# An FFT with a SiLU network on one core: first steps in direct form, later weights prepared between them

## The chip, the cores and the metric

One core of one Trainium2 chip runs the kernel in one launch. The metric is the device time in microseconds. Three runs of the kernel before took 938.07, 939.1 and 939.98 us; the median is 939.1.

## The reference

```python
X = np.fft.fft(np.fft.fft(x, axis=1), axis=2).real   # x: (4, 3008, 256)
x = X.astype(np.float32).reshape(4 * 3008, 256)
h = x @ w_in                                         # w_in: (256, 2048)
g = h * (1.0 / (1.0 + np.exp(-h)))
out = (g @ w_out).astype(np.float32)                 # w_out: (2048, 256)
```

Both weights are float64. The kernel gets their 64-bit words and makes float32 of them itself.

## The kernel before, in words

The Fourier transform over the 256 columns is folded into w_in: eight quarters q of 256 columns of w_in are each converted (`to_f32`, L66: an absolute value on ACT, then four passes on DVE), multiplied by a small matrix dft on PE (`project`, L415, eight products), and split into a part that is exact in the short format (abh, `large`, L423, on ACT) and a remainder (abl, `small`, L432, on DVE). `large` also takes one row out of the product, sends it by a DMA to a128, and sets that row to zero. The Fourier transform over the 3008 rows is done by products with tables (te, to, t2) in 16 chunks of 376 or 378 output rows, four kinds of chunk for each of the four batches. Each chunk needs an operand (`operand`, L194: sums and differences of folded x), a transform on PE (L255), and `spread` (L291), which copies the transform into uvh and uvl and sends its row 0 to all partitions as ub.

A chunk then goes through 16 steps f, one for 128 hidden columns. `first` (L309) makes two products u and v with six matmuls; `act` (L324) makes p = ub * a128 + u, p + v and p - v on DVE, which are h for a row and for its mirror row, and Silu and a short copy gh on ACT; gl = h - gh is a DVE pass in `rest` (L344), for chunk 0 a POOL pass in `act` (L341). `second` (L351), three steps later (LAG), multiplies by w_out with twelve matmuls into four accumulators, which `o` copies out after the last step.

All instructions of an engine run in the order in which the program writes them. Before the loop, a startup (L439 to L507) is written out by hand: loads of w_in and x on SyncE's queue, the second half of x added by a POOL DMA, tables by POOL, and the eight quarters, the first sums of x and the transform of chunk 0 laced into each other. Quarters 6 and 7 are projected there and copied in steps 0 and 1. In chunk 0, w_out's eight pieces are converted between the steps, one in two steps, by generators that `act` advances (`fill`). Two lists of generators, one for DVE work and one for POOL work (`queue`, `pool_queue`), are advanced a little at the end of each step by `drain`, with a budget; `plan` says at which step something is put on them. A tile of a pool with a tag has as many buffers as `bufs` says; a new one waits until the oldest is read.

Of the kernel before, what the change touches and what calls it, by code (L numbers as in the profile page):

```python
# [48 lines left out]
def fft_mlp(ctx, tc, x1, x2, w_in, w_out, te, to, t2, rot1, rot2, dft, out):  # L49
# [38 lines left out]

    def load_wo(q):

        wo_raw[q] = fold_p.tile([128, 2, D], I64, tag="ri0", name="wo", bufs=2)
        nc.sync.dma_start(out=wo_raw[q], in_=w_out[q * 256:(q + 1) * 256, :].rearrange("(f p) d -> p f d", p=128))  # L92

    def convert_wo(q):
        wf = fold_p.tile([128, 2, D], F32, tag="half", name="wf", bufs=3)
# [3 lines left out]
        yield
        tt(wl, wf, wh.bitcast(F32), op=ALU.subtract)  # L100

    def start_wo(q):
        wo_work[q] = convert_wo(q)
        next(wo_work[q])
# [293 lines left out]
    late = ctx.enter_context(ExitStack())  # L398
    with ExitStack() as start:
        st = start.enter_context(tc.tile_pool(name="st", bufs=1))  # L400
        wr = start.enter_context(tc.tile_pool(name="wr", bufs=3))
        ps = late.enter_context(tc.tile_pool(name="ps", bufs=2, space=PSUM))
        dft_sb = st.tile([128, 2, 2, 128], F32, name="dft_sb")
        win, wf32, pws, conv = {}, {}, {}, {}

        def load_w(q):
            win[q] = wr.tile([128, 2, 256], I64, tag="win", name="win", bufs=7)
            nc.sync.dma_start(out=win[q], in_=w_in[:, q * 256:(q + 1) * 256].rearrange("(c p) f -> p c f", p=128))

        def ahead(q):  # L410
            wf32[q] = wr.tile([128, 2, 256], F32, tag="wf", name="wf", bufs=3)
            conv[q] = to_f32(win.pop(q), wf32[q])
            next(conv[q])

        def project(q):  # L415

            w = wf32.pop(q)
            pw = pws[q] = pq_tile() if q in (1, 3, 5) else ps.tile([128, 2, 512], F32, tag="ps", name="pw")
            for m in range(2):
                for c in range(2):  # L420
                    nc.tensor.matmul(pw[:, m, :256], dft_sb[:, c, m, :], w[:, c], start=c == 0, stop=c == 1)

        def large(q):  # L423
            fs = slice(q * 256, (q + 1) * 256)
            pool, tag = (st, "row") if q < 6 else (fold_p, "half")
            row = pool.tile([1, 128, 2], F32, tag=tag, name="row", bufs=3)
            nc.scalar.activation(row, pws[q][0:1, 1, :256].rearrange("o (f p) -> o p f", p=128), AF.Copy)
            nc.sync.dma_start(out=a128[q], in_=row)
            nc.scalar.activation(pws[q][0:1, 1, :256], zero, AF.Copy)
            nc.scalar.activation(abh[:, :, fs], pws[q][:, :, :256], AF.Copy)  # L430

        def small(q):  # L432
            fs = slice(q * 256, (q + 1) * 256)
            tt(abl[:, :, fs], pws.pop(q)[:, :, :256], abh[:, :, fs].bitcast(F32), op=ALU.subtract)

        def load_tables(n, t):
            nc.gpsimd.dma_start(out=tabs[n], in_=t)

        load_w(0)  # L439
        load_w(1)  # L440
        nc.scalar.dma_start(out=dft_sb, in_=dft)
        nc.gpsimd.memset(zero, 0.0)
        warm = st.tile([1, 1], F32, name="warm")
        nc.scalar.activation(warm, zero[:, :1], AF.Silu)
        load_x(1, 0, lo)
        load_w(2)
        load_x(0, 0)
        add_x(1, 0, lo)
        add_x(0, 0)
        load_tables("t2", t2)  # L450
        for q in range(3, 8):
            load_w(q)
        nc.sync.dma_start(out=rot_sb[0], in_=rot1)
        nc.sync.dma_start(out=rot_sb[1], in_=rot2)
        load_wo(0)
        load_wo(1)

        ahead(0)
        ahead(1)
        run(conv.pop(0))  # L460
        project(0)
        ahead(2)
        run(conv.pop(1))
        large(0)
        project(1)
        run(conv.pop(2))
        large(1)
        small(0)
        project(2)
        ahead(3)  # L470
        run(first_sums(1, lo))
        large(2)
        small(1)
        small(2)
        run(conv.pop(3))
        project(3)
        ahead(4)
        large(3)
        run(first_sums(0))
        op = operand(0)  # L480
        for _ in range(3):
            next(op)
        run(conv.pop(4))
        run(op)
        project(4)
        po = pq_tile()
        ahead(5)
        ahead(6)
        large(4)
        small(3)  # L490
        run(conv.pop(5))
        transform(0, po)
        small(4)
        project(5)
        ahead(7)
        run(conv.pop(6))
        spread(0, po)
        project(6)
        large(5)
        small(5)  # L500
        run(conv.pop(7))
        project(7)
        load_tables("te", te)
        load_tables("to", to)
        start_wo(0)
        run(wo_work.pop(0))
        start_wo(1)  # L507
# [41 lines left out]
    for n in range(len(steps) + LAG):  # L549
# [6 lines left out]
        if n < len(steps):  # L556
# [6 lines left out]
        if n == 0:
            large(6)
            large(7)
        elif n == 1:
            small(6)
            small(7)
# [6 lines left out]
        if n < len(steps):  # L575
# [109 lines left out]
```

## Time and profile before

| | |
|---|---|
| median of three runs | 939.1 us |
| profiled execution, own time | 938.11 us |
| its span | 936.3 us |
| PE busy | 885.2 us, 95% |
| PEld busy | 873.0 us, 93% |
| DVE busy | 756.4 us, 81% |
| ACT busy | 534.4 us, 57% |
| POOL busy | 196.0 us, 21% |
| mean PE clock granted | 0.974 |

The span is the time from the first to the last instruction of one profiled execution. Busy times are shares of it; an engine can be far from busy over the whole span and still hold up a stretch of it. The clock is given as a share of 2.4 GHz; the lower of the two levels, 1.2 GHz, shows as 0.5.

### The profile page before, as it was taken

Reading aid. Unit: us, or ns where it says so; the run is one execution under the profiler, and the core shown is the slowest. Engines: PE = TensorE matmul, PEld = TensorE weight load, DVE = VectorE, ACT = ScalarE, POOL = GpSimd, SP = SyncE. Lnnn points to the kernel's source line nnn. Section 1 sums busy time; section 2 is a strip of 40 time slices with the busy share of each in tenths; the row PEclk is TensorE's granted clock in tenths of the full one; section 3 lists DMA queues with packets and bytes.
Section 4 is the critical chain, followed back from the end, with each engine's and each line's share of the span. In section 5 each row is a group of like instructions: output and inputs, shape, how many; then the busy total and the mean of one; then the engine's idle time right before and its main releaser. Section 6 shows DMA issues by size and latency. Waiting matters only on the chain.

```text
span 936.3 us, 12926 instructions
## 1 busy us (share of the span) xinstructions
PE 885.2 (95%) x5008; PEld 873.0 (93%) x5008; DVE 756.4 (81%) x1215; ACT 534.4 (57%) x738; POOL 196.0 (21%) x214
## 2 busy tenths in 40 slices
PE   3569979999989999999999999999999999999998
PEld 2458869999989999999999999999999999999998
DVE  5689868797877979797987879797887978797785
ACT  3245566565674656575755646475655656565554
POOL 1016562165040106080200106130000101010000
PEclk9579989999999999999999999999999999999999
DMA  9631311532102045210302033110302020120300
GB/s 268 250 54 41 55 36 25 78 78 8 35 0 23 21 95 127 7 37 1 42 1 10 34 54 79 6 37 1 42 1 9 34 9 34 5 38 1 43 1 34
DMA packets 19709, 40.96 MB, mean 44 GB/s; under 512 B 3264, under 2 KB 13504, under 8 KB 17728
## 3 DMA queue, kind: packets, MB, share of 16 engines
q1 hardware_dynamic: 18192, 30.12, 18.1%
q0 software_dynamic: 1312, 9.76, 4.5%
q8 instruction: 39, 0.64, 0.3%
q10 hardware_dynamic: 144, 0.26, 0.1%
q14 instruction: 22, 0.18, 0.1%
HBM read 24.70 MB, written 12.34 MB: 40 GB/s over the span
## 4 chain that ended last, share of the span: by engine, by line
PE 83%; DVE 7%; DMA 3%; ACT 2%; POOL 2%; issue 1%; SPq 1%; DVEq 0%; POOLq 0%; ACTq 0%
PE acc L360 17%; PE acc L365 17%; PE acc L361 17%; PE pq L317 9%; PE pq L316 9%; PE pq L315 9%; PE pq L269 5%; DMA a<-row 1%; DMA win<-in_w_in_dram 1%; SPq L92 1%; DVE h L328 1%; DVE h L331 1%; DVE wf L81 1%; DVE wf L79 1%; DVE h L332 1%
## 5 line engine op out<-in xcount | busy, mean ns | idle before, releaser
L338 ACT ACTIVATE h<-h 128x752 f32<-128x752 f32 (+2 forms) x258 | 213.8, 829 | 300.4 <-DVE h L332 298.0
L360 PE MATMUL acc<-gh,woh 128*128 128x376 f32 (+1 forms) x1024 | 345.6, 337 | 8.2 <-ACT o L373 5.4
L361 PE MATMUL acc<-gh,wol 128*128 128x376 f32 (+1 forms) x1024 | 345.0, 337 | 1.1 <-DVE wol L100 1.1
L349 DVE TENSOR_TENSOR gl<-h,gh 128x752 fp32r<-128x752 f32 (+2 forms) x242 | 236.4, 977 | 7.6 <-ACT gh L339 7.4
L365 PE MATMUL acc<-gl,woh 128*128 128x376 f32 (+1 forms) x1024 | 227.6, 336 | 0.0
L339 ACT ACTIVATE gh<-h 128x752 fp32r<-128x752 f32 (+2 forms) x258 | 214.2, 830 | 8.2
L328 DVE SCALAR_TENSOR_TENSOR h<-ub,a,pq 128x376 f32<-128x376 f32 (+1 forms) x256 | 154.6, 604 | 60.8 <-PE pq L317 58.7
L360 PEld LDWEIGHTS acc<-gh,woh 128*128 128x128 f32 x1024 | 194.0, 189 | 10.1 <-ACT o L373 5.7
L361 PEld LDWEIGHTS acc<-gh,wol 128*128 128x128 f32 x1024 | 194.5, 190 | 2.2 <-DVE wol L100 2.2
L365 PEld LDWEIGHTS acc<-gl,woh 128*128 128x128 f32 x1024 | 182.8, 190 | 0.0
L315 PE MATMUL pq<-uvh,abh 128*128 128x376 f32 (+1 forms) x512 | 173.6, 339 | 6.1 <-DVE h L332 5.7
L317 PE MATMUL pq<-uvh,abl 128*128 128x376 f32 (+1 forms) x512 | 173.1, 338 | 0.0
L316 PE MATMUL pq<-uvl,abh 128*128 128x376 f32 (+1 forms) x512 | 172.7, 337 | 0.0
L332 DVE TENSOR_TENSOR h<-h,pq 128x376 f32<-128x376 f32 (+1 forms) x256 | 140.1, 547 | 8.8
L331 DVE TENSOR_TENSOR h<-h,pq 128x376 f32<-128x376 f32 (+1 forms) x256 | 139.9, 546 | 8.4
L247 POOL TENSOR_TENSOR xl<-xf,xh 128x256 fp32r<-128x256 f32 x53 | 48.9, 948 | 325.5 <-ACT xh L240 157.5
L315 PEld LDWEIGHTS pq<-uvh,abh 128*128 128x128 f32 x512 | 97.4, 190 | 8.7 <-DVE h L332 7.6
L316 PEld LDWEIGHTS pq<-uvl,abh 128*128 128x128 f32 x512 | 97.5, 191 | 0.1
L317 PEld LDWEIGHTS pq<-uvh,abl 128*128 128x128 f32 x512 | 97.5, 190 | 0.0
L303 DVE TENSOR_TENSOR uvl<-pq,uvh 128x752 fp32r<-128x752 f32 (+1 forms) x16 | 15.1, 943 | 59.1 <-ACT uvh L302 59.1
L189 POOL TENSOR_TENSOR ri<-ri,raw 128x256 f32<-128x256 f32 (+1 forms) x28 | 26.0, 942 | 137.9 <-ACT ri L185 137.6
L341 POOL TENSOR_TENSOR gl<-h,gh 128x752 fp32r<-128x752 f32 x16 | 30.0, 1876 | 76.4 <-ACT gh L339 72.6
(83 smaller groups left out, 482.6 us busy)
## 6 DMA issues: line engine op xcount, KB each, us to landing
out_dram<-o SPq DMA_DIRECT2D x48, 188.0 KB, 2.3
raw<-in_x_dram SPq DMA_DIRECT2D x5, 1024.0 KB, 11.0
raw<-in_x_dram POOLq DMA_DIRECT2D x5, 1024.0 KB, 9.5
win<-in_w_in_dram SPq DMA_DIRECT2D x8, 512.0 KB, 13.7
wo<-in_w_out_dram SPq DMA_DIRECT2D x8, 512.0 KB, 4.0
out_dram<-o SPq DMA_DIRECT2D x16, 189.0 KB, 2.5
ub<-row SPq DMA_DIRECT2D x12, 188.0 KB, 8.5
t<-in_t_dram POOLq DMA_DIRECT2D x1, 1128.0 KB, 13.8
```

The lines of the kernel that those rows point to most:

```text
L315: nc.tensor.matmul(po, abh[:, i, fs], uvh[:, i, :n], start=True, stop=False)
L316: nc.tensor.matmul(po, abh[:, i, fs], uvl[:, i, :n], start=False, stop=False)
L317: nc.tensor.matmul(po, abl[:, i, fs], uvh[:, i, :n], start=False, stop=True)
L328: stt(p[:, :n], ub[:, :n], a128[f // 2][:, f % 2:f % 2 + 1], pq[:, 0, :n], op0=ALU.mult, op1=ALU.add)
L331: tt(h[:, 0, :n], p[:, :n], pq[:, 1, :n], op=ALU.add)
L332: tt(h[:, 1, :n], p[:, :n], pq[:, 1, :n], op=ALU.subtract)
L338: nc.scalar.activation(h[:, sg, :n], h[:, sg, :n], AF.Silu)
L339: nc.scalar.activation(gh[:, sg, :n], h[:, sg, :n], AF.Copy)
L349: tt(gl[:, sg, :n], g[:, sg, :n], gh[:, sg, :n].bitcast(F32), op=ALU.subtract)
L360: nc.tensor.matmul(po, wo[0][f // 2][:, f % 2, es], gh[:, sg, :n], start=f == 0, stop=False)
L361: nc.tensor.matmul(po, wo[1][f // 2][:, f % 2, es], gh[:, sg, :n], start=False, stop=False)
L365: nc.tensor.matmul(accs[c][i][:, :n], wo[0][f // 2][:, f % 2, es], gl[:, sg, :n], start=False, stop=f == NF - 1)
```

## The change

In the first eight steps of chunk 0 (`DIRECT = 8`), `first` makes h of both signs on PE by twelve matmuls: the first operand with v and with -v (vneg, made by ACT in `spread`). Row 0 of the second part keeps its sign (turn) and abh keeps the row in which a128 was taken (not set to zero for quarters 0 to 3), so DVE's three passes and a128 are not used there; ACT's Silu reads the products. After step 8 the row is set to zero in abh and abl by POOL.

```diff
+        if c == 0 and f < DIRECT:
+            for i, (vh, vl) in enumerate(((uvh[:, 1], uvl[:, 1]), (vneg[:, 0], vneg[:, 1]))):
+                for m, (oh, ol) in enumerate(((uvh[:, 0], uvl[:, 0]), (vh, vl))):
+                    for p, (a, x) in enumerate(((abh, oh), (abh, ol), (abl, oh))):
+                        nc.tensor.matmul(pq[:, i, :n], a[:, m, fs], x[:, :n], start=m + p == 0, stop=m + p == 3)
+            return
...
-            nc.scalar.activation(h[:, sg, :n], h[:, sg, :n], AF.Silu)
+            nc.scalar.activation(h[:, sg, :n], (pq if direct else h)[:, sg, :n], AF.Silu)
...
-        if c == 0:
-            nc.gpsimd.tensor_tensor(gl[:, :, :n], h[:, :, :n], gh[:, :, :n].bitcast(F32), op=ALU.subtract)
...
-        if NF < n <= len(steps):
+        if 1 <= n <= len(steps):
             rest(*steps[n - 1])
```

The startup loads x first and prepares quarters 0 to 3 and the product of quarter 4 (three buffers for w_in, where there were seven). The small rows (a, and ub of chunk 0) are sent by ACT's queue. w_out's first two pieces come by POOL's queue, te and to in step 8. The order of the startup is now, with the loads left out:

```diff
+    ahead(0)
+    run(conv.pop(0))
+    project(0)
+    large(0)
+    run(first_sums(1, lo))
+    small(0)
+    ahead(1)
+    run(conv.pop(1))
+    project(1)
+    ahead(2)
+    large(1)
+    run(first_sums(0))
+    small(1)
+    op = operand(0)
+    for _ in range(3):
+        next(op)
+    run(conv.pop(2))
+    project(2)
+    ahead(3)
+    run(op)
+    large(2)
+    small(2)
+    po = pq_tile()
+    transform(0, po)
+    run(conv.pop(3))
+    project(3)
+    ahead(4)
+    spread(0, po)
+    large(3)
+    small(3)
+    run(conv.pop(4))
+    project(4)
```

The other quarters, and w_out, are prepared between the steps (`late_w` is called behind `act` and ahead of `rest`):

```diff
+    def late_w(q):
+        if q > 4:
+            run(conv.pop(q))
+            project(q)
+        large(q)
+        if q < 7:
+            ahead(q + 1)
+        small(q)
...
-            act(c, f, (2 + f % 2) * (wo_work[max(f // 2, 1)],) if c == 0 else ())
+            act(c, f, (3 if f < DIRECT else 1) * (wo_work,) if c == 0 else ())
+        if n < LAG:
+            for q in ((4, 5), (6,), (7,))[n]:
+                late_w(q)
+        if n == LAG - 1:
             late.close()
```

w_out's remainder wl is made by POOL and not by DVE. Its conversion is one generator for all eight pieces (four advances each), and the load of a piece is issued when the piece two before it is converted. The lists change in three places:

```diff
-            pool_queue.append((("x", c), low()))
+            pool_queue.insert(0, (("x", c), low()))
...
-        at(c, {1: 8, 3: 6}.get(c, 0), add, queue, ("op", c + 1), operand(c + 1))
+        at(c, {1: 10, 3: 6}.get(c, 0), add, queue, ("op", c + 1), operand(c + 1))
...
-    at(0, 15, add, pool_queue, ("t2d", 0), fold_diffs(1, 0, lo))
-    at(0, 15, add, pool_queue, ("t1d", 0), fold_diffs(0, 0))
+    at(1, 0, add, pool_queue, ("t2d", 0), fold_diffs(1, 0, lo))
+    at(1, 0, add, pool_queue, ("t1d", 0), fold_diffs(0, 0))
...
-            drain(pool_queue, 1.2 if c == 1 else 0.6)
+            drain(pool_queue, 1.1 if c == 1 else 0.6)
```

## Rows read from the trace of the kernel before

**Rows 1.** Windows: length; PE, PEld, DVE, ACT, POOL busy us (instructions); PE clock; DMA; GB/s

```profile
56.20:68.70 12.50, 6.41 (x27) 5.24 (x25) 10.52 (x17) 6.77 (x12) 3.06 (x5) 0.77 0.21 64
68.70:120.10 51.40, 48.35 (x258) 44.76 (x259) 45.61 (x75) 28.39 (x39) 28.72 (x18) 0.95 0.25 50
120.10:145.00 24.90, 18.58 (x91) 17.57 (x91) 16.21 (x26) 15.26 (x29) 14.67 (x19) 0.86 0.20 54
256.00:285.00 29.00, 26.01 (x142) 25.20 (x140) 19.73 (x35) 19.94 (x33) 13.15 (x20) 0.95 0.01 1
400.00:600.00 200.00, 200.00 (x1169) 200.00 (x1168) 171.24 (x273) 120.52 (x163) 51.37 (x58) 1.00 0.18 30
```

**Rows 2.** Timeline of ACT in the startup: start us, us, instruction, idle time before it

```profile
0.74 0.45 ACTq L441 DMA_DIRECT2D dft_sb<-in_dft_dram  x1
38.92 0.37 ACT L427 ACTIVATE row<-pq 1x256 f32<-1x256 f32 x1 [18.53 <-DMA a<-row]
49.62 0.60 ACT L430 ACTIVATE abh<-pq 128x512 fp32r<-128x512 f32 x1
```

**Rows 3.** Timeline of SyncE's queue in the startup

```profile
14.38 12.02 SPq L92 DMA_DIRECT2D wo<-in_w_out_dram  x2
26.49 16.48 SPq L428 DMA_DIRECT2D a<-row  x5
```

**Rows 4.** Timeline of PE, startup and first chunk

```profile
32.77 3.75 PE L421 MATMUL pw<-wf,dft_sb 128*128 128x256 f32 x8 [3.90 <-DVE wf L81]
41.12 4.13 PE L269 MATMUL pq<-t,xh 128*128 128x376 f32 x12 [4.60 <-ACT xh L240]
46.88 1.89 PE L421 MATMUL pq<-wf,dft_sb 128*128 128x256 f32 x8
56.23 0.88 PE L315 MATMUL pq<-uvh,abh 128*128 128x376 f32 x1
68.69 0.65 PE L360 MATMUL acc<-gh,woh 128*128 128x376 f32 x1 [1.09 <-ACT gh L339]
120.10 0.33 PE L315 MATMUL pq<-uvh,abh 128*128 128x378 f32 x1
```

**Rows 5.** DMA issues of the first 60 us: count, KB each, us to landing

```profile
raw<-in_x_dram POOLq DMA_DIRECT2D x1, 1024.0 KB, 10.9
raw<-in_x_dram POOLq DMA_DIRECT2D x1, 512.0 KB, 8.1
to<-in_to_dram POOLq DMA_DIRECT2D x1, 1128.0 KB, 19.6
```

**Rows 6.** Timeline of DVE in the startup

```profile
24.95 1.21 DVE L156 TENSOR_TENSOR raw<-raw 128x1016 f32<-128x1016 f32 x1
28.54 0.42 DVE L202 TENSOR_TENSOR xf<-sm 128x258 f32<-128x258 f32 x1
30.28 0.43 DVE L75 TENSOR_SCALAR wf<-wf 128x512 f32<-128x512 f32 x1
30.75 0.43 DVE L77 TENSOR_SCALAR wf<-wf 128x512 uint32<-128x512 uint32 x1
31.93 0.69 DVE L81 SCALAR_TENSOR_TENSOR wf<-win,wf 128x512 uint32<-128x512 uint32 x1
```

**Rows 7.** Groups of DVE by form, 57 to 130 us: busy us, mean ns of one

```profile
L77 DVE TENSOR_SCALAR wf<-wf 128x512 uint32<-128x512 uint32 x7 | 7.3, 1036 | 0.0
```

**Rows 8.** Costliest groups of the page, whole span

```profile
L349 DVE TENSOR_TENSOR gl<-h,gh 128x752 fp32r<-128x752 f32 (+2 forms) x242 | 236.4, 977 | 7.6 <-ACT gh L339 7.4
L339 ACT ACTIVATE gh<-h 128x752 fp32r<-128x752 f32 (+2 forms) x258 | 214.2, 830 | 8.2
L341 POOL TENSOR_TENSOR gl<-h,gh 128x752 fp32r<-128x752 f32 x16 | 30.0, 1876 | 76.4 <-ACT gh L339 72.6
```

**Rows 9.** Waits of PE, whole span: us in total, times, longest

```profile
PE acc L360 <- ACT o L373: 5.4, 1, 5.4
PE pq L269 <- POOL xl L247: 3.0, 3, 2.5
```

More of the change, by code (lines that the diff above doesn't have):

```diff
@@ L39 @@
 LAG = 3
+DIRECT = 8
 PIECES = ((slice(0, 4),), (slice(0, 2), slice(2, 4)))
@@ L65, in fft_mlp @@
     zero = wts.tile([1, 256], F32, name="zero")
+    turn = wts.tile([128, 1], F32, name="turn")
+    vneg = fold_p.tile([128, 2, CH], F32R, tag="ri1", name="vneg")
     def to_f32(raw, dst):
@@ L83, in fft_mlp, with load_wo @@
     wo = [[wts.tile([128, 2, D], F32R, name=f"wo{p}{f}") for f in range(NF // 2)] for p in "hl"]
-    tabs = {n: wts.tile([128, 2, 3, 376], F32R, name=n) for n in ("te", "to", "t2")}
+    tabs = {"t2": wts.tile([128, 2, 3, 376], F32R, name="t2")}
     rot_sb = [wts.tile([128, 2, 2], F32, name=f"rot_sb{i}") for i in range(2)]
-    wo_raw, wo_work = {}, {}
-    def load_wo(q):
+    wo_raw = {}
+    def load_wo(q, queue=nc.sync):
         wo_raw[q] = fold_p.tile([128, 2, D], I64, tag="ri0", name="wo", bufs=2)
-        nc.sync.dma_start(out=wo_raw[q], in_=w_out[q * 256:(q + 1) * 256, :].rearrange("(f p) d -> p f d", p=128))
+        queue.dma_start(out=wo_raw[q], in_=w_out[q * 256:(q + 1) * 256, :].rearrange("(f p) d -> p f d", p=128))
     def convert_wo(q):
@@ L98, in convert_wo, with convert_all_wo @@
         nc.scalar.activation(wh, wf, AF.Copy)
[L99 to L104, printed above, removed]
+        nc.gpsimd.tensor_tensor(wl, wf, wh.bitcast(F32), op=ALU.subtract)
+    def convert_all_wo():
+        work = convert_wo(0)
+        next(work)
+        for q in range(NF // 2):
+            yield from work
+            if q + 2 < NF // 2:
+                load_wo(q + 2)
+            if q + 1 < NF // 2:
+                work = convert_wo(q + 1)
+                next(work)
+            yield
     def run(work):
@@ L300, in spread @@
         nc.scalar.activation(row[:, :n], po[0:1, 1, :n], AF.Copy)
-        nc.sync.dma_start(out=ub[:, :n], in_=row[:, :n].unsqueeze(0).to_broadcast([1, 128, n]))
+        (nc.sync if c else nc.scalar).dma_start(out=ub[:, :n], in_=row[:, :n].unsqueeze(0).to_broadcast([1, 128, n]))
         nc.scalar.activation(uvh[:, :, :n], po[:, :, :n], AF.Copy)
@@ L304, in spread @@
         chunks[c] = uvh, uvl, ub, n, o
+        if c == 0:
+            for p, uv in enumerate((uvh, uvl)):
+                nc.scalar.activation(vneg[:, p, :n], uv[:, 1, :n].bitcast(F32), AF.Copy, scale=turn[:, :])
     pqs, gs, accs = {}, {}, {}
@@ L327, in act @@
         p = h[:, 1]
-        stt(p[:, :n], ub[:, :n], a128[f // 2][:, f % 2:f % 2 + 1], pq[:, 0, :n], op0=ALU.mult, op1=ALU.add)
+        direct = c == 0 and f < DIRECT
+        if not direct:
+            stt(p[:, :n], ub[:, :n], a128[f // 2][:, f % 2:f % 2 + 1], pq[:, 0, :n], op0=ALU.mult, op1=ALU.add)
         for work in fill[:1]:
             next(work, None)
-        tt(h[:, 0, :n], p[:, :n], pq[:, 1, :n], op=ALU.add)
-        tt(h[:, 1, :n], p[:, :n], pq[:, 1, :n], op=ALU.subtract)
+        if not direct:
+            tt(h[:, 0, :n], p[:, :n], pq[:, 1, :n], op=ALU.add)
+            tt(h[:, 1, :n], p[:, :n], pq[:, 1, :n], op=ALU.subtract)
         for work in fill[1:]:
@@ L396, in drain @@
                 budget -= cost
[L398 to L507, printed above, removed]
@@ L509, in fft_mlp, with load_w @@
     gp = ctx.enter_context(tc.tile_pool(name="gp", bufs=LAG))
     mp = ctx.enter_context(tc.tile_pool(name="mp", bufs=2))
+    late = ctx.enter_context(ExitStack())
+    wr = late.enter_context(tc.tile_pool(name="wr", bufs=1))
+    ps = late.enter_context(tc.tile_pool(name="ps", bufs=2, space=PSUM))
+    dft_sb = wr.tile([128, 2, 2, 128], F32, name="dft_sb")
+    win, wf32, pws, conv = {}, {}, {}, {}
+    def load_w(q):
+        win[q] = wr.tile([128, 2, 256], I64, tag="win", name="win", bufs=3)
+        nc.sync.dma_start(out=win[q], in_=w_in[:, q * 256:(q + 1) * 256].rearrange("(c p) f -> p c f", p=128))
@@ new lines, in ahead, with project, large @@
+    def ahead(q):
+        wf32[q] = wr.tile([128, 2, 256], F32, tag="wf", name="wf", bufs=2)
+        conv[q] = to_f32(win.pop(q), wf32[q])
+        next(conv[q])
+    def project(q):
+        w = wf32.pop(q)
+        pw = pws[q] = pq_tile() if q in (1, 3) else ps.tile([128, 2, 512], F32, tag="ps", name="pw")
+        for m in range(2):
+            for c in range(2):
+                nc.tensor.matmul(pw[:, m, :256], dft_sb[:, c, m, :], w[:, c], start=c == 0, stop=c == 1)
+    def large(q):
+        fs = slice(q * 256, (q + 1) * 256)
+        row = fold_p.tile([1, 128, 2], F32, tag="half", name="row", bufs=3)
+        nc.scalar.activation(row, pws[q][0:1, 1, :256].rearrange("o (f p) -> o p f", p=128), AF.Copy)
+        nc.scalar.dma_start(out=a128[q], in_=row)
+        if 2 * q >= DIRECT:
+            nc.scalar.activation(pws[q][0:1, 1, :256], zero, AF.Copy)
+        nc.scalar.activation(abh[:, :, fs], pws[q][:, :, :256], AF.Copy)
@@ new lines, in small, with load_tables @@
+    def small(q):
+        fs = slice(q * 256, (q + 1) * 256)
+        tt(abl[:, :, fs], pws.pop(q)[:, :, :256], abh[:, :, fs].bitcast(F32), op=ALU.subtract)
+    def load_tables(n, t):
+        nc.gpsimd.dma_start(out=tabs[n], in_=t)
+    load_x(1, 0, lo)
+    load_w(0)
+    load_x(0, 0)
+    nc.scalar.dma_start(out=dft_sb, in_=dft)
+    nc.gpsimd.memset(zero, 0.0)
+    nc.gpsimd.memset(turn, -1.0)
+    nc.gpsimd.memset(turn[0:1], 1.0)
+    warm = wr.tile([1, 1], F32, name="warm")
+    nc.scalar.activation(warm, zero[:, :1], AF.Silu)
@@ new lines, in fft_mlp @@
+    add_x(1, 0, lo)
+    add_x(0, 0)
+    load_tables("t2", t2)
+    load_wo(0, nc.gpsimd)
+    load_wo(1, nc.gpsimd)
+    for q in range(1, 8):
+        load_w(q)
+    nc.sync.dma_start(out=rot_sb[0], in_=rot1)
+    nc.sync.dma_start(out=rot_sb[1], in_=rot2)
+    ahead(0)
[12 more added lines that the diff above has]
+    op = operand(0)
@@ L561, in fft_mlp @@
                 transform(c + 1, new)
-            act(c, f, (2 + f % 2) * (wo_work[max(f // 2, 1)],) if c == 0 else ())
[L563 to L568, printed above, removed]
+            act(c, f, (3 if f < DIRECT else 1) * (wo_work,) if c == 0 else ())
[3 more added lines that the diff above has]
+        if n == LAG - 1:
             late.close()
             acc_p = ctx.enter_context(tc.tile_pool(name="acc", bufs=1, space=PSUM))
-        if NF < n <= len(steps):
+            tabs_p = ctx.enter_context(tc.tile_pool(name="tabs", bufs=1))
+        if c == 0 and f == DIRECT:
+            for name, t in (("te", te), ("to", to)):
+                tabs[name] = tabs_p.tile([128, 2, 3, 376], F32R, name=name)
+                load_tables(name, t)
+            for a in (abh, abl):
+                nc.gpsimd.memset(a[0:1, 1, :DIRECT * 128].bitcast(F32), 0.0)
+        if 1 <= n <= len(steps):
             rest(*steps[n - 1])
```

7 lines of the change are left out of this document (2 added, 5 removed).

## The prediction

> **What bounds the kernel now.** I read the busy table by windows first, then the timeline of each engine up to 145 us, then PE's waits. The reader is to see that the kernel has two parts. From some 145 us on PE is never idle: between 400 and 600 us its 1169 matmuls fill all 200 us, 0.171 us each, with DVE at 86% [rows 1]. Nothing in the change shortens that. What is left to win lies before: PE's first product of the network is at 56.2 us, the first product with w_out at 68.7, and the second chunk begins at 120.1 [rows 4]. The startup is held by one wait: ACT sits idle 18.5 us until 38.9 for a buffer whose small row (a) has not been sent [rows 2], because SyncE's queue was 12.0 us in issuing two w_out loads and sent the first row only at 26.5 [rows 3]. From 68.7 to 120.1 DVE is busy 45.6 of 51.4 us and PE could have done its 258 matmuls in 258 x 0.171 = 44.1. Two later stretches lose time as well: 120.1 to 145 (91 matmuls, 15.6 us of work in 24.9: 9.3 lost, of which 5.4 is a wait for o) and 256 to 285 (142 matmuls, 24.3 in 29.0: 4.7 lost, 3.0 of it a wait for POOL's xl) [rows 1, 9]. The rest of the loss is the cold clock after each wait: the mean grant is 0.86 and 0.95 there [rows 1].
>
> **Prices.** Converting a quarter of w_in on DVE: 30.28 to 31.93 + 0.69, 2.3 us [rows 6]. Its eight products with dft: 3.75 us where PE had been idle and 1.89 right behind other products [rows 4]. `large`: row 0.37, the row's DMA now issued by ACT itself (the one that ACT issues in the trace takes 0.45), zeroing 0.4 where it is kept, copy 0.60: 1.4 or 1.8 us [rows 2]. `small`: one DVE pass over 512 columns, 0.7, as the last pass of the conversion [rows 6]. Silu and the copy: 2 x 0.83; gl: 0.98 on DVE, 1.88 on POOL [rows 8]; wl on POOL has 512 columns instead of 752, so about 1.3.
>
> **Part 1, up to the first product: 56.2 becomes 52.** The small rows leave SyncE's queue, so the 18.5 us go. What is late next is the chain of x and of the weights. x's first half is loaded and then added, 8.1 us each, so it is there at about 17; the larger part, issued just behind, needs 10.9 for the adding alone and is there near 23.5 [rows 5]. DVE: sums of the half to 20.6 (24.95 to 28.54 is 3.6), small(0) and conversion 1 to 23.6. Then conversion, product, `large` and `small` follow each other: product 1 to 27.4, copy to 28.8, small(1) to 29.5 (the sums of the second part lie beside), operand 1.7 (28.54 to 30.28 [rows 6]) to 31.2, conversion 2 to 33.5, product 2 to 37.3. The transform takes 18 products: 5.8 us cold (41.12 to 46.88 [rows 4]), 3.1 at 0.171; PE has just worked, so I take 4: it ends at 41. Behind it row 0.4, DMA issue 0.45, uvh 0.8, uvl 0.95, the negated copy 0.5, `large`(3) 1.4, small(3) 0.7, conversion 4 2.3, and product 4 cold 3.75, which stands ahead of the first product in PE's order: 11.2 us, 52. Bounds: 47 (loads 2 us earlier, products 1.89) and 56 (nothing gained).
>
> **Part 2, steps 0 to 2: 12.5 us become 44.** Before, steps 0 to 2 took 56.2 to 68.7 [rows 4], with all eight weights projected. Now `late_w` puts weights 5, 6 and 7 between the steps, and each engine takes its instructions in the written order. `run(conv)` on DVE, `project` on PE, `large` on ACT and `small` on DVE wait for each other, and DVE's next conversion stands behind `small`; PE's next `first` stands behind `project`, the w_out pieces behind `small`. From the first product on: twelve products 2.8 (between 12 x 0.171 and half speed), silu and copy to 4.5, large(4) 6.4, small(4) 7.1, conversion 5 9.4, product 5 (PE idle since 2.8, cold) 13.2, large(5) 15.1, small(5) 15.8, the two sums of z 17.0. Step 1: the last w_out pass, its copy on ACT 0.6, wl on POOL 1.3 and then ACT's 0.65, which needs wl's buffer (three under that tag): 20.3; two passes 21.2, conversion 6 23.5, product 27.3, large and small 29.9, gl and xf 31.9. Step 2: two passes, copy, ACT, one pass 35.0, conversion 7 37.3, product 41.1, large 42.9, small 43.6. Only then are the acc banks free, so the first product with w_out is at about 44. PE's own work in this is 36 x 0.171 + 3 x 1.89 = 12 us, so 32 of the 44 are waits. Bounds: 38 with every product at 1.89, 47 with `first` cold too.
>
> **Part 3, steps 3 to 15: 51.4 become 48.** The direct form adds 6 products to eight steps, 48 x 0.171 = 8.2 us of PE, 5.1 of them here at most in steps 3 to 7; it takes three passes of 376 columns off DVE there, and gl (16 x 0.98) comes to DVE. PE: second(0) 12, four steps of 24, eight of 18 are 252 x 0.171 = 43.1, and the next transform's 30 at most 5.1: 48.2. DVE in a direct step: three w_out passes, about 1.7, and gl 0.98, against PE's 4.1, so gl costs nothing there; from step 8 on it is about 3.1 against 3.1, with LAG as slack. Bounds 46 and 51. Issued from step 8 on, te and to have 15 us until the transform; `to` took 19.6 to land in the crowded startup [rows 5], so up to 4 us could stick out; I take none, since the queues are empty then.
>
> What the row shows of POOL beside DVE: the pass L77 takes 0.43 alone [rows 6] and 1.04 in the mean while POOL makes gl [rows 7]. The Trainium skill (Perfetto Trace Analysis, Optimizing Scalar/DVE Operations) says that the two share an SBUF read port, so that moving work from one to the other might not help. By that rule wl on POOL would stretch a pass in steps 1 and 2 by 0.6 each and the sum would be 1 us higher; the sum here leaves it out.
>
> **Part 4, after 120.1: 13.3 us less.** POOL is no longer behind with gl, the fold of diffs begins a step later, and o is copied ahead of the ACT copies scaled by rot: of the 9.3 us lost there I take 9.1 back. xl is put at the head of POOL's list: the 4.7 us near 280 go. Operand 2 begins two steps later (10 for 8), so xl of chunk 2 is just in time: 0.5 back. Bounds of the part: 9 and 14.
>
> **Sum.** 52 + 44 + 48.2 = 144.2 for the start of chunk 1, 24.1 later than 120.1; less 13.3: 10.8 later. The profiled execution took 938.1 us (span 936.3, 1.8 around it), so 948.9; the median of the runs is 1.0 above that execution: 950. Its own range, from the terms' bounds not all on one side, is 943 to 958.
>
> **Rivals.** *The clock stays up (chance 0.14).* Place: products 1, 2, 4 to 7 and the transform. If PE is granted 2.4 GHz through the gaps, each `project` costs 1.89, the startup ends at 47, steps 0 to 2 take 38, and the sum is 950 - 5 - 6 - 1 = 938: not slower. It decides from about 10 us saved, that is, when nearly all of them are at 1.89. For: product 4 of before ran at 1.89 behind a transform. Against: the products that followed 3.9 us of idle PE took 3.75 [rows 4], and here each follows 3 to 7 us. *The weights are hidden beside the steps (0.06).* If the conversions ran ahead of the copies as in the old startup, steps 0 to 2 would be PE's 12 us: 950 - 32 = 918. Against: the written order, and that ACT before kept to it: it stood 18.5 us at one row [rows 2] with all its later work behind. *Worse (0.16).* No gain in the startup (56), 47 for steps 0 to 2, 4 us of waiting for `to`, and half of part 4 kept back: 950 + 4 + 3 + 4 + 3 = 964; for it speaks that x is read, added and waited for on one path now.
>
> **How the numbers follow.** Forecast 0.64. The range 938 to 960 holds it, half of the clock's case and part of the worse one. A measurement of this kernel can tell 0.2%, 1.9 us, from no change. Faster: 0.06 for hidden weights and 0.06 of the clock's case, 0.12; same: 0.07, most of the rest of that case; slower 0.81.
>
> **What would show it.** In the changed profile: ACT has no wait of over 10 us for a's DMA; PE's first product of the network lies near 52; three products with dft stand behind it, each with PE idle for 3 to 7 us before it, on DVE's last pass; ACT's `row` in `large` waits for PE there, and DVE's `small` for ACT; the first product with w_out lies near 96; steps 4 to 7 run at 24 products in 4.1 us; the waits for o and for xl are gone. It is wrong if the first w_out product lies before 85, or if the second chunk begins before 135.

## The result, and the profile after

The changed kernel takes 944.8 us (median of 4 runs, 944.83 to 945.08), beside 938.6 for the kernel before in the same group of runs (936.5 to 939.98): a ratio of 1.0069, 95% interval [1.0049, 1.0089], slower by 0.7%. The profiled execution has a span of 942.9 us against 936.3, 6.6 longer, at a mean granted clock of 0.975 (0.974 before).

First the timeline of PE (start, us, instruction, idle time before it and what ended it), which answers to [rows 4].

```profile
46.38 3.78 PE L441 MATMUL pw<-wf,dft_sb 128*128 128x256 f32 x8 [4.59 <-DVE wf L84]
49.60 0.88 PE L332 MATMUL pq<-uvh,abh 128*128 128x376 f32 x1
...
59.79 3.78 PE L441 MATMUL pw<-wf,dft_sb 128*128 128x256 f32 x8 [6.57 <-DVE wf L84]
...
73.27 3.38 PE L441 MATMUL pw<-wf,dft_sb 128*128 128x256 f32 x8 [6.53 <-DVE wf L84]
...
87.23 3.75 PE L441 MATMUL pw<-wf,dft_sb 128*128 128x256 f32 x8 [8.53 <-DVE wf L84]
...
93.94 0.33 PE L380 MATMUL acc<-gh,woh 128*128 128x376 f32 x1
...
141.07 0.34 PE L336 MATMUL pq<-uvh,abh 128*128 128x378 f32 x1
```

The first product of the network is at 49.60 (56.23 before), the first with w_out at 93.94 (68.69), chunk 1 begins at 141.07 (120.10). Between the first two stand the three products with dft of weights 5, 6 and 7, each behind 6.5 to 8.5 us of idle PE, and each released by DVE's last conversion pass. So the start is 21.0 us longer. What follows is 942.9 - 141.07 = 801.8 us against 936.3 - 120.1 = 816.2: 14.4 shorter. 21.0 - 14.4 = 6.6, the whole difference.

The windows (length; PE, PEld, DVE, ACT, POOL busy us with instructions; PE clock; DMA share; GB/s), which answer to [rows 1]:

```profile
49.00:93.00 44.00, 22.37 (x71) 19.18 (x71) 16.02 (x29) 13.96 (x25) 2.52 (x2) 0.66 0.11 33
93.00:141.00 48.00, 48.00 (x288) 47.89 (x287) 41.86 (x65) 27.46 (x37) 14.36 (x14) 1.00 0.39 97
140.00:165.00 25.00, 25.00 (x147) 25.00 (x146) 22.42 (x34) 19.19 (x34) 12.53 (x17) 1.00 0.19 54
256.00:310.00 54.00, 54.00 (x315) 54.00 (x314) 45.61 (x79) 34.33 (x50) 11.12 (x16) 1.00 0.15 19
```

In the first row PE is busy half the time and every other engine less, and the granted clock is down at 0.66: engines waiting for each other in turn. In the three rows from 93 us on PE is never idle, at clock 1.00, where the clock in the windows of [rows 1] stood at 0.95, 0.86 and 0.95. PE's waits over the whole span (us, times, longest) say it once more, against [rows 9]: the wait for o is gone, 0.2 us is left of those for xl, and all the rest is the last pass of a conversion.

```profile
PE pw L441 <- DVE wf L84: 43.1, 6, 10.5
PE pq L441 <- DVE wf L84: 8.5, 2, 6.9
PE pq L280 <- POOL xl L258: 0.2, 1, 0.2
```

One turn of the ring, from the product of quarter 5 to that of quarter 6, on ACT:

```profile
63.60 0.37 ACT L446 ACTIVATE row<-pw 1x256 f32<-1x256 f32 x1 [6.31 <-PE pw L441]
64.01 0.48 ACTq L447 DMA_DIRECT2D a<-row  x1
64.53 0.38 ACT L449 ACTIVATE pw<-zero 1x256 f32<-1x256 f32 x1 [0.55 <-ACT row L446]
64.94 0.60 ACT L450 ACTIVATE abh<-pw 128x512 fp32r<-128x512 f32 x1
...
68.62 0.64 ACT L76 ACTIVATE wf<-wo 128x512 f32<-128x512 f32 x1
```

on DVE:

```profile
65.57 0.69 DVE L454 TENSOR_TENSOR abl<-pw,abh 128x512 fp32r<-128x512 f32 x1 [5.83 <-ACT abh L450]
...
69.30 1.12 DVE L78 TENSOR_SCALAR wf<-wf 128x512 f32<-128x512 f32 x1 [1.24 <-ACT wf L76]
...
72.44 0.69 DVE L84 SCALAR_TENSOR_TENSOR wf<-win,wf 128x512 uint32<-128x512 uint32 x1
```

and on POOL, which makes w_out's remainder wl:

```profile
68.87 1.26 POOL L102 TENSOR_TENSOR wol<-wf,woh 128x512 fp32r<-128x512 f32 x1 [35.71 <-ACT woh L101]
```

PE 59.79 to 63.57, ACT to 65.54, DVE to 73.13, PE again at 73.27: a turn of 13.48 us, the next 13.96. ACT's wait of 6.31 ends on PE, DVE's 5.83 on ACT, PE's 6.53 on DVE: on the way from one product to the next the engines work one after the other. Some work lies beside that way (PE's twelve products of step 1 from 63.01, ACT's Silu), but it does not shorten it. DVE's part, 7.6 us, also holds two sums of z, three passes for w_out and a wait of 1.24 for ACT; the conversion of quarter 6 itself begins only at 70.79.

### The profile page after: what moved, and what is told of

The parts are those of the page before. It is cut to its first block, busy times and chain, and to the rows that moved or that the text cites. A ratio compares the mean times of both kernels' runs of the same rounds, so it can differ in the third digit from the quotient of the medians.

```text
span 942.9 us, 12965 instructions
## 1 busy us (share of the span) xinstructions
PE 887.7 (94%) x5056; PEld 879.2 (93%) x5056; DVE 748.0 (79%) x1199; ACT 534.3 (57%) x736; POOL 183.9 (20%) x212
## 4 chain that ended last, share of the span: by engine, by line
PE 87%; DVE 6%; ACT 3%; DMA 1%; issue 1%; ACTq 0%; POOL 0%; DVEq 0%
PE acc L385 18%; PE acc L381 18%; PE acc L380 18%; PE pq L336 9%; PE pq L337 9%; PE pq L338 8%; PE pq L280 5%; PE pw L441 2%; PE pq L332 2%; DMA raw<-in_x_dram 1%; DVE gl L369 1%; DVE wf L84 1%; DVE wf L82 1%; PE pq L441 1%; ACT h L360 1%
## 5 line engine op out<-in xcount | busy, mean ns | idle before, releaser
L360 ACT ACTIVATE h<-h 128x752 f32<-128x752 f32 (+2 forms) x250 | 207.3, 829 | 290.9 <-DVE h L354 288.4
L369 DVE TENSOR_TENSOR gl<-h,gh 128x752 fp32r<-128x752 f32 (+2 forms) x258 | 254.9, 988 | 3.5 <-ACT gh L361 3.3
L349 DVE SCALAR_TENSOR_TENSOR h<-ub,a,pq 128x376 f32<-128x376 f32 (+1 forms) x248 | 150.0, 605 | 56.7 <-PE pq L338 54.8
L336 PE MATMUL pq<-uvh,abh 128*128 128x376 f32 (+1 forms) x496 | 166.6, 336 | 0.0
L337 PE MATMUL pq<-uvl,abh 128*128 128x376 f32 (+1 forms) x496 | 166.2, 335 | 0.0
L338 PE MATMUL pq<-uvh,abl 128*128 128x376 f32 (+1 forms) x496 | 166.0, 335 | 0.0
L354 DVE TENSOR_TENSOR h<-h,pq 128x376 f32<-128x376 f32 (+1 forms) x248 | 135.7, 547 | 8.5
L353 DVE TENSOR_TENSOR h<-h,pq 128x376 f32<-128x376 f32 (+1 forms) x248 | 135.6, 547 | 8.3
L337 PEld LDWEIGHTS pq<-uvl,abh 128*128 128x128 f32 x496 | 93.5, 189 | 0.0
L441 PE MATMUL pw<-wf,dft_sb 128*128 128x256 f32 x48 | 22.2, 644 | 43.1 <-DVE wf L84 43.1
L441 PEld LDWEIGHTS pw<-wf,dft_sb 128*128 128x128 f32 x48 | 15.1, 329 | 48.3 <-DVE wf L84 29.5
```

What stands on the lines that cost most here:

```text
L336: nc.tensor.matmul(po, abh[:, i, fs], uvh[:, i, :n], start=True, stop=False)
L337: nc.tensor.matmul(po, abh[:, i, fs], uvl[:, i, :n], start=False, stop=False)
L338: nc.tensor.matmul(po, abl[:, i, fs], uvh[:, i, :n], start=False, stop=True)
L360: nc.scalar.activation(h[:, sg, :n], (pq if direct else h)[:, sg, :n], AF.Silu)
L369: tt(gl[:, sg, :n], g[:, sg, :n], gh[:, sg, :n].bitcast(F32), op=ALU.subtract)
```

## The experiments

Spans below are of the profiled executions; the changed kernel's is 942.9. A ratio is to the kernel before in the same group of runs; its median was 936.97 to 938.59 us from group to group, so a difference of some 2 us between runs of different groups is not told from noise by the times alone. Every kernel computes the whole result.

**The ring taken apart (e_ahead).** Conversions 5 and 6 run before step 0, conversion 7 in it; the product of quarter 5 follows step 0, those of 6 and 7 step 1. The direct form and its 48 added products stay.

```diff
+    for q in (5, 6):
+        ahead(q)
+        run(conv.pop(q))
+    ahead(7)
...
+    def late_w(n):
+        if n == 0:
+            project(5)
+            run(conv.pop(7))
+            large(4)
+            large(5)
+            small(4)
+            small(5)
+        elif n == 1:
+            project(6)
+            project(7)
+            large(6)
+            large(7)
+            small(6)
+            small(7)
```

> The changed kernel with the conversions of quarters 5, 6 and 7 taken out of the chain: DVE converts 5 and 6 in its idle time ahead of step 0 and 7 in step 0, project(5) stands behind step 0's products, 6 and 7 behind step 1's, each small behind all conversions; four wf buffers for two. All 48 added products stay. Serial-chain theory: steps 0 to 2 take some 20 us instead of 44.3, PE's first product with w_out lies near 70 instead of 93.9, time 920 us (914 to 927), faster than both kernels. Rival, that the 48 added products (8.2 us on the busiest engine) are the loss: 940 or more, as they are all still there.

Measured: 924.1 us, ratio 0.9862 [0.9848, 0.9877], span 922.2; the first product with w_out at 67.51, chunk 1 at 120.36, 801.8 us of rest as in the changed kernel. Its PE timeline:

```profile
51.91 1.89 PE L441 MATMUL pw<-wf,dft_sb 128*128 128x256 f32 x8
...
57.17 3.72 PE L441 MATMUL pw<-wf,dft_sb 128*128 128x256 f32 x16 [1.31 <-DVE abl L454]
...
67.51 0.44 PE L380 MATMUL acc<-gh,woh 128*128 128x376 f32 x1 [2.50 <-DVE abl L454]
```

The products with dft now take 1.89 for one and 3.72 for two, and from step 0 on no wait of PE is above 2.7. The first product of the network comes where it did (49.66). So the place of the three conversions and their products costs the changed kernel 942.9 - 922.2 = 20.7 us of span; the added products, all still there, do not.

**The clock in the ring (e_warm).** Thirty useless products ahead of each of products 5, 6 and 7; nothing else differs.

```diff
     def project(q):
...
+        if q > 4:
+            uvh = chunks[0][0]
+            for k in range(30):
+                nc.tensor.matmul(pw[:, k % 2, :376], abh[:, 0, :128], uvh[:, 0, :376], start=True, stop=True)
```

> The changed kernel with 30 products more, of no use, put ahead of each of project(5), (6) and (7), into the same PSUM tile, so that PE is busy while it waits for the conversion. Serial-chain theory with its cold products: the three projects take 1.9 instead of 3.4 to 3.8 us and the twelve products behind each run at 0.171, so steps 0 to 2 shrink from 44.3 to 38 to 40 us: 939 to 941 us. If the clock were not part of the price: 945. If PE's amount of work were the bound (rival): 90 products of 0.171 more, 960.

Measured: 941.2 us, 1.0044 [1.0028, 1.006], span 938.5, just above what was expected. PE timeline:

```profile
52.98 5.31 PE L442 MATMUL pw<-uvh,abh 128*128 128x376 f32 x30
59.72 1.99 PE L445 MATMUL pw<-wf,dft_sb 128*128 128x256 f32 x8 [1.43 <-DVE wf L84]
...
71.37 2.65 PE L445 MATMUL pw<-wf,dft_sb 128*128 128x256 f32 x8 [2.47 <-DVE wf L84]
...
84.54 1.99 PE L445 MATMUL pw<-wf,dft_sb 128*128 128x256 f32 x8 [2.36 <-DVE wf L84]
...
89.29 0.44 PE L380 MATMUL acc<-gh,woh 128*128 128x376 f32 x1 [0.67 <-DVE abl L458]
```

Behind other work two of the products take 1.99 and one 2.65, where they took 3.38 to 3.78; from the first product to the first with w_out the granted clock is 0.93 (0.66 in the changed kernel), and the first product with w_out comes 4.65 us earlier. The span is 4.4 shorter (the median 3.6): about that much of the ring's price is the lower clock (not all of its price, since 0.93 is not 1.00), and the turns themselves are the rest.

**The direct form alone (e_ahead_d0).** e_ahead with `DIRECT = 0`: no vneg, h made by DVE as before, two advances of w_out's conversion a step.

```diff
-DIRECT = 8
+DIRECT = 0
...
-            act(c, f, (3 if f < DIRECT else 1) * (wo_work,) if c == 0 else ())
+            act(c, f, 2 * (wo_work,) if c == 0 else ())
```

> The kernel with the conversions taken out of the chain (924.1 us), without the direct form: DIRECT 0, six products and DVE's three passes in every step, w_out converted in two advances a step, vneg and the clearing of its row left out. By the rows DVE then has 2.53 + 1.15 = 3.7 us in a step and PE 3.1, where the direct form has 4.14 of PE in eight steps and 3.1 in the others: 16 x 3.7 against 8 x 4.14 + 8 x 3.1, 59 against 58, so 925 us (921 to 929): the direct form is worth next to nothing by itself. Rival, that relief of DVE is what the direct form brings (24 passes of 0.55, 13 us): 936.

Measured: 929.2 us, 0.9908 [0.9888, 0.9928], span 927.8: 5.6 longer than e_ahead, just above the expected range. Of PE's waits (us, times, longest) the largest of those that e_ahead has smaller or not at all:

```profile
PE acc L378 <- DVE abl L452: 4.8, 1, 4.8
PE pw L439 <- DVE abl L452: 4.7, 1, 4.7
PE acc L379 <- POOL wol L101: 4.5, 6, 0.9
```

In this order the direct form is worth some 5 us. The two waits for DVE's abl are 9.5 us where e_ahead has 3.8, so the reading is that the direct form frees DVE while PE waits for it; but 1.6 of the 5.6 us lie ahead of the first product (51.26 for 49.66), and the shares were not tried apart.

**The lists (e_append, e_fold).** In e_append xl goes to the end of POOL's list again; in e_fold the fold of diffs begins at (0, 15) again.

```diff
-            pool_queue.insert(0, (("x", c), low()))
+            pool_queue.append((("x", c), low()))
```

> The changed kernel with xl's generator put at the end of POOL's list again (append for insert). By part 4 of the prediction the wait for xl near 280 us comes back, 4.7 us lost with its cold products: 949 to 950 us. If the order of the list does not matter, because the fold now begins a step later anyway: 945.

Measured: 950.8 us, 1.0145 [1.013, 1.016], span 949.3: 6.4 longer, a little more than was expected. Chunk 1 begins at 140.98, as in the changed kernel, so all of it lies behind. The wait of [rows 9] is back at its old size, and the window from 256 to 300 us has a clock of 0.92 where the changed kernel shows 1.00:

```profile
PE pq L280 <- POOL xl L258: 2.9, 3, 2.5
```

```profile
256.00:300.00 44.00, 41.22 (x220) 40.27 (x219) 32.02 (x54) 28.45 (x45) 13.18 (x20) 0.92 0.11 21
```

```diff
-    at(1, 0, add, pool_queue, ("t2d", 0), fold_diffs(1, 0, lo))
-    at(1, 0, add, pool_queue, ("t1d", 0), fold_diffs(0, 0))
+    at(0, 15, add, pool_queue, ("t2d", 0), fold_diffs(1, 0, lo))
+    at(0, 15, add, pool_queue, ("t1d", 0), fold_diffs(0, 0))
```

> The changed kernel with the fold of diffs begun at step 15 of chunk 0 again, the rest as changed (gl on DVE). If POOL's being behind with gl made the wait for o (5.4 us and the cold products behind it), that wait stays away and only the ACT copies scaled by rot, now ahead of o again, cost something: 945 to 948 us. If the early fold alone made it: the 7 us come back, 952.

Measured: 948.5 us, 1.0115 [1.0098, 1.0133], span 946.4: 3.5 longer, just above the first of the two sizes expected. ACT's timeline shows why: eight copies scaled by rot (150.06 to 153.26; the first here) stand ahead of o, and PE waits 2.3 us for it.

```profile
150.06 0.50 ACT L195 ACTIVATE raw<-raw,rot_sb 64x256 f32<-64x256 f32 x1
...
153.26 1.57 ACT L393 ACTIVATE o<-acc 128x376 f32<-128x376 f32 x4
```

**gl on POOL again (e_glpool).**

```diff
+        if c == 0:
+            nc.gpsimd.tensor_tensor(gl[:, :, :n], h[:, :, :n], gh[:, :, :n].bitcast(F32), op=ALU.subtract)
...
-        if 1 <= n <= len(steps):
+        if NF < n <= len(steps):
             rest(*steps[n - 1])
```

> The changed kernel with one part undone: gl of chunk 0 is made by POOL again, as before the change; nothing else differs. Theory (the chain through the projections sets the first 94 us, and from step 4 on PE's products set the end, so where gl is made decides nothing): 945, range 943 to 947, and chunk 1 begins within 1 us of 141.1. Rival (POOL's gl takes 1.88 us where DVE's takes 0.98, on the one queue that also holds wl, te and to, so that the products with w_out or the last steps of chunk 0 come later): 949 to 952, with a new wait of PE for gl or for o of several us.

Measured: 949.6 us, 1.0132 [1.0115, 1.0149], span 946.9, 4.0 longer: the theory fell, the rival's size holds, its wait does not (none for gl or o). The first product with w_out comes 1.0 later (94.92), chunk 1 begins 4.4 later (145.48). On DVE, two passes of the conversions are long beside POOL's gl, which is the next fence:

```profile
70.24 1.87 DVE L80 TENSOR_SCALAR wf<-wf 128x512 uint32<-128x512 uint32 x1
...
85.40 2.14 DVE L82 SCALAR_TENSOR_TENSOR wf<-win,wf 128x512 uint32<-128x512 uint32 x1
```

```profile
69.89 1.94 POOL L363 TENSOR_TENSOR gl<-h,gh 128x752 fp32r<-128x752 f32 x1 [0.76 <-ACT gh L361]
...
85.12 1.88 POOL L363 TENSOR_TENSOR gl<-h,gh 128x752 fp32r<-128x752 f32 x1 [0.84 <-ACT gh L361]
```

In the changed kernel these two passes take 0.43 and 0.69. Each starts 0.3 us after POOL's gl and ends 0.3 and 0.5 us after it: 1.4 us lost twice, on the one path there is. Part of it comes back, since gl's own 0.93 is off DVE there. Of the further 3.4 us up to chunk 1, PE's waits show 1.6 for a silu, 0.4 for uvl and 0.2 for h; POOL also issues te and to only from 123.89 (from 116.58 in the changed kernel). How the rest divides was not tried.

**The small rows alone (e_rows), and x first (e_xfirst).** The kernel before, with a's rows and the first ub sent by ACT's queue; then the same with x loaded ahead of the weights.

```diff
-        nc.sync.dma_start(out=ub[:, :n], in_=row[:, :n].unsqueeze(0).to_broadcast([1, 128, n]))
+        (nc.sync if c else nc.scalar).dma_start(out=ub[:, :n], in_=row[:, :n].unsqueeze(0).to_broadcast([1, 128, n]))
...
-            nc.sync.dma_start(out=a128[q], in_=row)
+            nc.scalar.dma_start(out=a128[q], in_=row)
```

> The kernel before with one part of the change alone: the small rows a and the first ub issued by ACT's queue. By part 1 the 18.5 us wait of ACT goes; PE's transform then starts behind project(4) at about 36.5 instead of 41.1, the first product of the network comes at about 50.5 instead of 56.2, and as chunk 0 is bound by DVE from there on all of it is kept: 933 us (931 to 936). Rival, that x's chain and DVE are as late anyway: 937 to 939.

Measured: 931.8 us, 0.9944 [0.9928, 0.9961], span 929.3. ACT's wait of 18.5 us [rows 2] has become one of 8.6 for PE:

```profile
29.18 0.37 ACT L427 ACTIVATE row<-pq 1x256 f32<-1x256 f32 x1 [8.59 <-PE pq L421]
```

The first product of the network lies at 49.5, as in the changed kernel, but with all eight quarters projected; chunk 1 begins at 112.7. So the queue of the small rows alone brings all that the changed startup gains; x first and three quarters put off add nothing to it together (x first alone is the next run; the quarters put off alone were not tried).

```diff
+        load_x(1, 0, lo)
...
+        load_x(0, 0)
...
-        load_x(1, 0, lo)
...
-        load_x(0, 0)
```

> The kernel with the small rows on ACT's queue alone (931.8 us), and x loaded first as in the change (x's first half, w_in 0, the rest of x, w_in 1). Theory: DVE was not held by x in that order but by its own passes, so the order of the loads is worth nothing: 932 us (930.5 to 933.5). Rival, that x first brings the transform forward: 929 or less.

Measured: 937.1 us, 0.9985 [0.9975, 0.9994], span 936.1: a miss, some 5 us slower than e_rows (its first product of the network comes 5.7 later, at 55.24). The quarters of w_in come late; ACT waits for each (its timeline; the same four waits in e_rows are 2.63, 1.10, 3.17 and none):

```profile
7.46 0.66 ACT L73 ACTIVATE wf<-win 128x512 f32<-128x512 f32 x1 [4.79 <-DMA win<-in_w_in_dram]
12.56 0.66 ACT L73 ACTIVATE wf<-win 128x512 f32<-128x512 f32 x1 [4.44 <-DMA win<-in_w_in_dram]
17.69 0.67 ACT L73 ACTIVATE wf<-win 128x512 f32<-128x512 f32 x1 [4.47 <-DMA win<-in_w_in_dram]
...
25.44 0.67 ACT L73 ACTIVATE wf<-win 128x512 f32<-128x512 f32 x1 [3.37 <-DMA win<-in_w_in_dram]
```

**The startup of before with all the rest of the change (e_old).** Eight quarters projected in the old order, rows on ACT's queue, direct form, gl on DVE, wl on POOL, the lists.

```diff
+        if c == 0 and f < DIRECT:
...
-        tt(wl, wf, wh.bitcast(F32), op=ALU.subtract)
+        nc.gpsimd.tensor_tensor(wl, wf, wh.bitcast(F32), op=ALU.subtract)
```

> The startup of the kernel before (all eight quarters converted and projected ahead of the loop, weights first and x behind them) with the small rows on ACT's queue, and all the rest of the change (direct form in eight steps, gl on DVE, wl on POOL, the lists). Serial-chain theory: the first product of the network stays at 49.5 us (as in the run with the rows alone), the first product with w_out comes near 61, the rest of chunk 0 takes 47 and the rest of the kernel 802 as in the changed kernel: span 910, 912 us (908 to 916). Rival, that loading x first was what brought the first product from 56.2 to 49.6: the first product at 56, 918 or more. Rival, that the added products are the loss: 940.

Measured: 922.9 us, 0.9845 [0.9825, 0.9864], span 921.0: 11 us above the expectation. 3.3 of them lie ahead of the first product of the network, which comes at 52.81 and not at 49.5; ACT's two copies for vneg (43.23 to 44.76) stand ahead of a `large` there. For the rest, ACT's timeline in steps 0 and 1 (before the silu at 61.52, `large` of 6 and 7 and w_out's copy, ten entries from 56.83):

```profile
55.26 0.80 ACT L363 ACTIVATE h<-pq 128x752 f32<-128x752 f32 x1 [8.13 <-PE pq L335]
...
56.83 0.36 ACT L450 ACTIVATE row<-pw 1x256 f32<-1x256 f32 x1
...
60.97 0.65 ACT L76 ACTIVATE wf<-wo 128x512 f32<-128x512 f32 x1
61.52 0.79 ACT L363 ACTIVATE h<-pq 128x752 f32<-128x752 f32 x1
```

PE waits 5.8 us in three waits for such a silu, and DVE's next pass waited 8.78 for the L76 in the third row. With the direct form PE's products need only ACT to go on, so what stands in ACT's queue ahead of a silu now holds PE; that ACT's order is the cause of the rest of the miss is read from this trace and was not tried by itself.

**The small parts put together (e_tail, e_tail_wl, e_tail_wl7).** No direct form. e_tail is e_rows with the three changes of the lists (and the budget of POOL's list in chunk 1 at 1.1 for 1.2, as in the change); e_tail_wl has wl on POOL too; e_tail_wl7 also runs conversion and product 7 ahead of `small`(5).

```diff
-            pool_queue.append((("x", c), low()))
+            pool_queue.insert(0, (("x", c), low()))
...
-        at(c, {1: 8, 3: 6}.get(c, 0), add, queue, ("op", c + 1), operand(c + 1))
+        at(c, {1: 10, 3: 6}.get(c, 0), add, queue, ("op", c + 1), operand(c + 1))
...
+    at(1, 0, add, pool_queue, ("t2d", 0), fold_diffs(1, 0, lo))
+    at(1, 0, add, pool_queue, ("t1d", 0), fold_diffs(0, 0))
```

> The kernel before with the small rows on ACT's queue (931.8 us) and the changes of the lists alone: xl at the head of POOL's list, the fold of diffs a step later, operand 2 two steps later; gl of chunk 0 stays on POOL. The wait for xl goes (4.7 us), the wait for o shrinks to 1 to 2 us as o is now copied ahead of the scaled copies: 921 us (918 to 924). If gl on POOL is what makes the wait for o, that wait stays: 927.

Measured: 921.0 us, 0.9824 [0.9805, 0.9842], span 918.6, 10.7 below e_rows. gl of chunk 0 is still made by POOL here, yet of PE's wait for o (5.4 in [rows 9]) only this is left:

```profile
PE acc L360 <- ACT o L373: 1.2, 1, 1.2
```

```diff
-        tt(wl, wf, wh.bitcast(F32), op=ALU.subtract)
+        nc.gpsimd.tensor_tensor(wl, wf, wh.bitcast(F32), op=ALU.subtract)
```

> The kernel before with the small rows on ACT's queue and the lists as changed (921.0 us), and one part more of the change: w_out's remainder wl made by POOL. Chunk 0 is bound by DVE there (45.7 of 51.5 us busy, and waits for the short copy before each wl): 7 passes of 0.69 and some of the waits go, POOL has room (29 of 51.5): 915 us (911 to 919), with no direct form at all. Rival, that POOL beside DVE stretches DVE's passes by what is saved (the shared port): 921.

Measured: 918.3 us, 0.9788 [0.9773, 0.9802], span 916.3. DVE's groups by form from 57 to 125 us (busy us, mean ns), of e_tail:

```profile
L81 DVE SCALAR_TENSOR_TENSOR wf<-wo,wf 128x512 uint32<-128x512 uint32 x7 | 7.8, 1110 | 0.0
L79 DVE SCALAR_TENSOR_TENSOR wf<-wo,wf 128x512 uint32<-128x512 uint32 x7 | 6.4, 921 | 0.0
L100 DVE TENSOR_TENSOR wol<-wf,woh 128x512 fp32r<-128x512 f32 x7 | 4.8, 692 | 4.9 <-ACT woh L98 4.9
```

and of e_tail_wl:

```profile
L79 DVE SCALAR_TENSOR_TENSOR wf<-wo,wf 128x512 uint32<-128x512 uint32 x7 | 11.5, 1642 | 0.0
L81 DVE SCALAR_TENSOR_TENSOR wf<-wo,wf 128x512 uint32<-128x512 uint32 x7 | 9.1, 1304 | 0.0
```

The seven passes of wl (4.8 us) and the wait ahead of them (4.9) leave DVE, but L79 and L81 grow by 6.4 us while POOL works on wl, and L77 shrinks (1371 to 714 ns, 3.9 us): some of what was moved comes back. Beside it e_old (span 921.0) has the direct form, gl on DVE, and w_out's conversion as one generator with te and to late: in the old startup these together cost 4.7 us of span, where the direct form saved 5.6 in e_ahead.

```diff
-        small(5)
...
+        small(5)
```

> The same, and in the startup conversion 7 and project(7) ahead of small(5) on DVE, which waits 0.9 us for ACT: the first product of the network some 1.3 us earlier, 914 us. If ACT or PE hold that product: the same as e_tail_wl.

Measured: 916.2 us, 0.9765 [0.975, 0.9779], span 914.7: the fastest of all, 2.3% below the kernel before, with none of the added products.

## Why the prediction was right

Slower was forecast, at 950 (938 to 960); it came at 944.8, and the mechanism is the forecast one: quarters 5 to 7 in a ring between the steps.

*Part 1 was the term mis-sized most: 52 forecast, 49.6 measured.* The chain was as forecast, but it began some 2.4 us earlier, because x's first half was there earlier. The prediction took x's transfers at the durations of [rows 5], where only the two adds are listed; the plain loads ahead of them were priced like these. The issues of the first 60 us (count, KB, us to landing) now show each:

```profile
raw<-in_x_dram POOLq DMA_DIRECT2D x1, 1024.0 KB, 10.4
...
raw<-in_x_dram SPq DMA_DIRECT2D x1, 512.0 KB, 5.4
raw<-in_x_dram POOLq DMA_DIRECT2D x1, 512.0 KB, 8.2
```

The adds took 8.2 and 10.4, near the 8.1 and 10.9 of the forecast; the plain load of the half took 5.4. DVE's sums began at 14.69 and, right behind its own passes, at 21.11, where 17 and 23.5 were forecast, and all that follows moved with them.

*Part 2: 44 forecast, 44.3 measured.* The ring is the forecast one, and the turns of 13.48 and 13.96 us answer to 14.1 and 13.8. e_ahead shows that the ring is the price, e_warm that its clock is about 4.4 of it. That the total agrees within 0.3 us is in part luck, for errors inside it cancel. The first twelve products took 3.6 us (49.60 to 53.22) and not 2.8. In step 1 the prediction lets ACT's pass over w_out wait 1.3 us for POOL's wl; it began at 68.62, before wl did, so that wait does not exist. PE's last gap, 8.53 us, is longer than the 3 to 7 named as a sign. And the prediction left out of the sum that a pass of DVE grows while POOL makes wl. In this trace it does: the L78 of the ring above takes 1.12 where it takes 0.42 alone, with POOL's wl from 68.87 to 70.13. The Trainium skill (Perfetto Trace Analysis, Optimizing Scalar/DVE Operations) says that the two share a read port, so that moving work between them might not help. DVE's passes do grow beside POOL in this trace, in e_glpool and in e_tail_wl, but the outcome went both ways: gl on POOL lost 4.0 us of span, wl on POOL won 2.3 net.

*Part 3: 48.2 forecast, 47.1 measured,* with PE busy 48.00 of 48.00 us from 93 to 141; a direct step of 24 products takes 4.15 us (96.02 to 100.17), as forecast, and the transform's 30 products take 3.5 (128.20 to 131.74) where at most 5.1 was taken. The late tables cost nothing, as taken. That gl on DVE costs nothing held, but "nothing" undersold it: undone, it is 4.0 us of span (e_glpool).

*Part 4: 13.3 forecast (9.1 and 4.7 gained, 0.5 given back), 14.4 measured.* The waits for o and for xl went with their cold clock; e_append and e_fold show 6.4 (for the 4.7) and 3.5 of it one at a time, and how the remaining 4.5 divide was not tried. The first reason given for the wait for o, POOL being behind with gl, is not borne out once the fold begins later: with gl on POOL again, e_glpool has no wait for o, and 801.4 us behind the start of chunk 1 as against 801.8. Beside the early fold it may still matter (5.4 us before, 2.3 in e_fold with gl on DVE).

*The rivals.* The clock stayed down in the ring (3.78, 3.38, 3.75 us a product). Hidden weights, forecast at 918, exist as e_ahead at 924.1; the written order of the change is not that. `to` was not late. In the rival called worse a sum is wrong: half of part 4 is 6.7 us and not 3, which would make it 968; the forecast does not use it.

In sum against the kernel before: -6.63 (49.60 - 56.23), +31.88 (44.34 - 12.46) and -4.28 (47.13 - 51.41) for parts 1 to 3, that is +20.97, and -14.4 behind. Of the 5 us between 950 and 944.8, the four parts make 4.3; the rest is the 1.0 that was added for a median above the profiled execution, and both were 944.8 here. The change contains a gain of 1.8% in its smallest edits (e_tail), and spends it on the ring.

## What to carry to other kernels

Before deferring work into a loop, follow one turn of it through the engines' written orders: where each engine's next instruction waits for the last of another, the work costs the sum of all engines' times and the cold clock besides, however idle they look. Move the first stage of such a chain one turn ahead of the rest, as e_ahead does. And try the small edits of a large change one at a time: here the queue of the small rows, the order of the lists and one engine's pass were worth more than the main idea.

## What the runs showed of the hardware that was not expected

A DMA issued by ACT in the ring takes 0.48 us of ACT's own time, and ACT computes nothing for 0.55 us in all between the instructions on either side of it; in e_rows that was cheap against a row held behind SyncE's loads. Loading x first looked free and was not: in e_xfirst ACT waited 3.4 to 4.8 us for each of the first four quarters, and the kernel lost some 5 us on e_rows. In e_glpool a DVE pass of 0.43 and one of 0.69 us that each met a 1.9 us POOL pass ended only 0.3 and 0.5 us after it (they took 1.87 and 2.14 us).
